# Second layer of a two-layer expert network: the gate as one Silu, low halves on VectorE, weight sets made across stage changes, first operands fetched in another order

## The chip, the cores and the metric

The kernel runs on one core of a Trainium2 chip. The metric is the device time of one execution in microseconds (us), as the median of several runs. The engines are TensorE (PE in the rows; its weight loads are PEld), VectorE (DVE), ScalarE (ACT), GpSimd (POOL) and SyncE (SP), which issues the DMAs of this kernel, in program order. Every engine takes its instructions in program order.

## The reference, cut to what matters

An attention block with 32 memory slots gives `x` of 4608 tokens by 512 features. Two layers of the same shape follow, 512 to 2048 and back to 512, in float32:

```python
def _moe_ref(x, w_in, w_out):       # first layer
    h = x @ w_in
    g = h * (1.0 / (1.0 + np.exp(-1.702 * h)))
    return g @ w_out

def _moe2_ref(x, w_in, w_out):      # second layer
    h = x @ w_in
    g = h * (1.0 / (1.0 + np.exp(-h)))
    return g @ w_out
```

## The kernel before, in words

Each float32 operand of a matmul is split in two: a rounded copy in the type F32R, written by ScalarE (the "high half"), and the remainder, a subtraction on VectorE or GpSimd (the "low half"). A product is then three matmuls (`PASSES`, L316). The last three of the four stages multiply 2x2 block matrices with seven products in place of eight; `ORDER` (L399) gives their order 1, 2, 6, 5, 7, 3, 4, and the price is sums and differences of operand blocks.

Four stages follow each other, in a schedule written out by hand: `at(slot, when, fn, ...)` enters a step in a table and `emit` issues it at its place, so the order of the calls is the order on each engine.

1. **First stage** (L336, 128 steps): attention and the first layer's first product. The gate is a Tanh on ScalarE and a multiply on VectorE (L338, L339). `store` (L342) sends each tile `g` to the DRAM tensors `g1s`. In the last twelve steps, from `ZS` (L956), `b_fetch` (L680) fetches the first operands of the second stage from `g1s`: 11 calls, 16 transfers of 384 KB, one call a step. `swap_pools` has by then given the attention's room to the pools `xst` (tags `xr0` to `xr6`) and `xp` (tags `x1` to `x7`).
2. **Second stage**, `middle` (L999; products at L734, 168 steps of 12 matmuls): the first layer's second product. `b_make` prepares the operand of step t+3 while step t runs (`AHEAD`, L970). At its start the pool `moe`, with the tiles that the last stores still read, is freed, and `b4` and `wm` take its room: `b_make(2)` writes into it. 12 weight sets are fetched (`wb_fetch`, L392). Towards its end, from L = T - 28, it makes weight sets of the third stage: `w_fetch` (L435) brings four 256 KB pieces into a staging tile (`wst` in the pool `wm`, or the tags `xr0` to `xr4`), and `w_make` forms sums (`w_sum`, L445), the high half (`w_hi`, L470) and the low half (`w_low`, L473). A set of weights for one chunk c has 7 of these. Then `x_fetch`, `x_comb` and `x_split` bring, combine and split the third stage's first operands (`xr` to `xq`).
3. **Third stage**, `step1` (L544; products at L521): the second layer's first product, 48 rounds n (`NG1`) of seven products of 6 matmuls, in 6 blocks of 384-token pairs with 8 rounds each. A round has seven places k. Copies of banks go to tiles `e` (L554, L571, L582), VectorE adds the second products (L408), `tanh` (L528) writes a tile `gq` on ScalarE, and `close` (L532) forms (tanh(h) + 1) * h on VectorE and stores the result to the DRAM tensors `gs`. The weights carry a factor one half, so h is half the true value. The operands of the next block are combined and split around the change of blocks (L1070 to L1077), in part on GpSimd. `c2_part` (L795) converts the raw `w_out` weights beside it, five small operations on ScalarE, VectorE and GpSimd for each of 16 pieces. In the last block the weight sets of the fourth stage are made (`spread`, L1052), odd low halves on GpSimd.
4. **Fourth stage** (L637, 168 steps of 18 matmuls): the second layer's second product. `r_fetch` (L591) fetches its operands from `gs`, `a_prep` (L614) splits them three steps ahead (`make`, L1101).

Before the first step of the fourth stage the pools `ps3`, `ps_y` and `m3` of the third are freed, and its PSUM pool `ps4` (4 buffers of two banks) takes the banks. In the kernel before, `x` (three buffers) is the first tag of `ps3` and `y1` the second.

Of the kernel before, what the change touches and what calls it, by code (L numbers as in the profile page):

```python
# [21 lines left out]
def attn_moe_moe(ctx: ExitStack, tc: tile.TileContext, q, k, v, phi, w1i, w1o, w2i, w2o, out):  # L22
# [24 lines left out]
    ones = const.tile([128, 1], F32)  # L47
    w2s = dram.tile([128, 2, 16, 512], F32, name="w2s")
# [465 lines left out]
    e1, e2, xb, y2, gq = {}, {}, {}, {}, {}  # L514
# [10 lines left out]
    def e_tile():  # L525
        return pools["m3"].tile([128, HB], F32, tag="e", name="e", bufs=6)

    def tanh(key, h):  # L528
        t = gq[key] = pools["m3"].tile([128, HB], F32, tag="gq", name="gq", bufs=8)
        nc.scalar.activation(out=t, in_=h, func=ACTF.Tanh)  # L530
# [13 lines left out]
    def step1(n, k):  # L544

        new, old = n < NG1, n > 0
        if k == 0 and new:
            xb[n] = pools["ps3"].tile([128, 512], F32, tag="x", name="xb", bufs=3)[:, :HB]
            prod1(n, 1, xb[n], True)
            e1[n] = e_tile()  # L550
        if k == 0 and old:
            tanh((n - 1, 1, 1), e2[n - 1, 2])
        if k == 0 and new:
            nc.scalar.copy(out=e1[n], in_=xb[n])  # L554
        if k == 0 and old:
            close(n - 1, 1, 1, e2.pop((n - 1, 2)))
        if k == 1 and new:
            y1 = pools["ps3"].tile([128, 512], F32, tag="y1", name="y1")[:, :HB]
            prod1(n, 2, y1, True)
            add(nc.vector, e1[n], e1[n], y1)  # L560
            tanh((n, 0, 0), e1[n])
# [10 lines left out]
        if k == 3 and old:  # L572
            close(n - 1, 0, 1, e2.pop(n - 1))
# [40 lines left out]
    def a_prep(b, i, p, then):  # L614
# [5 lines left out]
        pool, tag = (("xp", "x1"), ("xp", "x2"), ("wm", "wst"), ("m4", "op2"))[k]  # L620
# [20 lines left out]
    def o_tile():  # L641
        return pools["m4"].tile([128, TT, 256], F32, tag="o", name="o4", bufs=5)
# [356 lines left out]
    def middle():  # L999
# [25 lines left out]
        for i, k in ((6, 23), (5, 24), (7, 25), (1, 26), (2, 27)):  # L1025
# [15 lines left out]
    def second_layer():  # L1041
# [4 lines left out]
        pools["ps_y"] = tc.alloc_tile_pool(name="ps_y", bufs=1, space=PSUM, side="right", reuse_waits="tile")  # L1046
        pools["m3"] = tc.alloc_tile_pool(name="m3", bufs=1, reuse_waits="tile")
# [120 lines left out]
```

## Time and profile before

| | |
|---|---|
| median of 3 runs | 1538.79 us (1536.07 to 1541.72) |
| profiled execution: its own time | 1541.98 us |
| its span, first to last instruction | 1540.2 us |
| granted TensorE clock, mean | 0.98 |
| busy share of the span: PE, DVE, ACT, POOL | 93%, 76%, 51%, 29% |

The span is cut into stages by the first and last matmul of each line. "Busy" is the time in which an engine ran instructions; "idle before" is the time an engine waited ahead of a group, with the instruction that ended the wait. PEclk is the share of its full clock that TensorE was granted. Start times count from the span's start.

### The profile page before, as it was taken

Reading aid. Unit: us, or ns where it says so; the run is one execution under the profiler, and the core shown is the slowest. Engines: PE = TensorE matmul, PEld = TensorE weight load, DVE = VectorE, ACT = ScalarE, POOL = GpSimd, SP = SyncE. Lnnn points to the kernel's source line nnn. Section 1 sums busy time; section 2 is a strip of 40 time slices with the busy share of each in tenths; the row PEclk is TensorE's granted clock in tenths of the full one; section 3 lists DMA queues with packets and bytes.
Section 4 is the critical chain, followed back from the end, with each engine's and each line's share of the span. In section 5 each row is a group of like instructions: output and inputs, shape, how many; then the busy total and the mean of one; then the engine's idle time right before and its main releaser. Section 6 shows DMA issues by size and latency. Waiting matters only on the chain.

```text
span 1540.2 us, 27551 instructions
## 1 busy us (share of the span) xinstructions
PE 1429.7 (93%) x10432; PEld 1346.2 (87%) x10432; DVE 1164.3 (76%) x1601; ACT 792.6 (51%) x1351; POOL 439.3 (29%) x292
## 2 busy tenths in 40 slices
PE   5579898889989999999989999999997999999998
PEld 3447777677779999999989999999997999999998
DVE  5777767676758888887987776767788788787875
ACT  3445656555634554554555655665564444444443
POOL 2322636363400011011002233333322044053150
PEclk9799999999999999999999999999998999999999
DMA  9657787867686366366233645455465515425230
GB/s 250 195 159 234 222 246 233 267 196 225 241 313 229 100 228 233 108 226 222 88 121 124 201 166 209 147 203 188 156 201 194 186 39 188 141 76 196 98 119 31
DMA packets 234438, 277.07 MB, mean 180 GB/s; under 512 B 52033, under 2 KB 218945, under 8 KB 234305
## 3 DMA queue, kind: packets, MB, share of 16 engines
q1 hardware_dynamic: 234304, 275.31, 54.6%
q8 instruction: 82, 1.34, 0.3%
q14 instruction: 52, 0.42, 0.1%
HBM read 166.20 MB, written 109.05 MB: 179 GB/s over the span
## 4 chain that ended last, share of the span: by engine, by line
PE 66%; DVE 7%; DMA 5%; issue 4%; ACT 3%; POOL 3%; SPq 1%; DVEq 0%; ACTq 0%; POOLq 0%
PE p L637 24%; PE pb L734 20%; PE xb L521 9%; PE y L521 6%; PE h L336 5%; DMA g1s<-g 4%; POOL xq L411 1%; PE a L239 1%; DVE op L411 1%; DVE pm L145 1%; DVE g L339 1%; DVE wq L411 1%; ACT g L338 1%; DVE e L408 1%; ACT gq L530 1%
## 5 line engine op out<-in xcount | busy, mean ns | idle before, releaser
L637 PE MATMUL p<-wq,op 128*128 128x256 f32 x3024 | 362.1, 283 | 4.8 <-DVE gq L535 4.8
L637 PEld LDWEIGHTS p<-wq,op 128*128 128x128 f32 x3024 | 361.9, 192 | 5.2 <-DVE gq L535 5.2
L734 PE MATMUL pb<-op,wq 128*128 128x384 f32 x2016 | 355.9, 338 | 9.3 <-ACT op L713 5.6
L734 PEld LDWEIGHTS pb<-op,wq 128*128 128x128 f32 x2016 | 352.6, 189 | 12.4 <-ACT op L713 6.3
L411 DVE TENSOR_TENSOR op<-rr,op 128x768 fp32r<-128x768 f32 x216 | 247.9, 1157 | 67.4 <-ACT op L622 41.8
L336 PE MATMUL h<-attnT,slab 128*128 128x288 f32 x1536 | 240.9, 310 | 17.6 <-DVE g L339 8.6
L336 PEld LDWEIGHTS h<-attnT,slab 128*128 128x128 f32 x1536 | 217.3, 196 | 45.3 <-DVE g L339 21.6
L521 PE MATMUL xb<-xq,wq 128*128 128x384 f32 x1152 | 219.2, 338 | 14.0 <-ACT e L554 5.6
L521 PEld LDWEIGHTS xb<-xq,wq 128*128 128x128 f32 x1152 | 199.9, 188 | 21.5 <-ACT e L554 8.7
L339 DVE SCALAR_TENSOR_TENSOR g<-g,h 128x288 f32<-128x288 f32 x256 | 106.9, 448 | 87.9 <-ACT g L338 86.8
L411 DVE TENSOR_TENSOR op<-r,op 128x768 fp32r<-128x768 f32 x120 | 131.3, 1101 | 54.7 <-ACT op L622 31.2
L521 PE MATMUL y<-xq,wq 128*128 128x384 f32 x864 | 165.7, 336 | 0.7 <-ACT e L582 0.7
L338 ACT ACTIVATE g<-h 128x288 f32<-128x288 f32 x256 | 99.0, 413 | 127.7 <-PE h L336 67.0
L813 POOL TENSOR_TENSOR c<-c 128x512 int32<-128x512 int32 x32 | 55.6, 1739 | 348.7 <-DVE c L810 140.8
L622 ACT CAST op<-rr 128x768 fp32r<-128x768 f32 x120 | 99.7, 835 | 107.1 <-PE p L637 81.4
L521 PEld LDWEIGHTS y<-xq,wq 128*128 128x128 f32 x864 | 151.1, 188 | 1.0 <-ACT e L582 1.0
L535 DVE SCALAR_TENSOR_TENSOR gq<-gq,e 128x384 f32<-128x384 f32 x144 | 113.2, 790 | 39.2 <-ACT gq L530 34.8
L530 ACT ACTIVATE gq<-e 128x384 f32<-128x384 f32 x144 | 75.3, 525 | 110.5 <-DVE e L408 108.0
L713 ACT CAST op<-rr 128x768 fp32r<-128x768 f32 x96 | 79.5, 833 | 71.5 <-PE pb L734 43.3
L408 POOL TENSOR_TENSOR rr<-rr,r 128x768 f32<-128x768 f32 x22 | 52.7, 2424 | 214.6 <-DMA r<-gs 214.6
L713 ACT CAST op<-r 128x768 fp32r<-128x768 f32 x72 | 60.0, 834 | 54.7 <-PE pb L734 44.8
L411 POOL TENSOR_TENSOR wq<-wst,wq 128x512 fp32r<-128x512 f32 x46 | 62.1, 1354 | 86.0 <-ACT wq L470 64.9
(110 smaller groups left out, 1541.2 us busy)
## 6 DMA issues: line engine op xcount, KB each, us to landing
g1s<-g SPq DMA_DIRECT2D x128, 288.0 KB, 4.3
gs<-gq SPq DMA_DIRECT2D x192, 192.0 KB, 2.1
rr<-g1s SPq DMA_DIRECT2D x60, 384.0 KB, 6.2
rr<-gs SPq DMA_DIRECT2D x60, 384.0 KB, 5.7
r<-g1s SPq DMA_DIRECT2D x36, 384.0 KB, 4.1
r<-gs SPq DMA_DIRECT2D x36, 384.0 KB, 6.1
xs<-eb SPq DMA_DIRECT2D x24, 384.0 KB, 3.1
xr<-xs SPq DMA_DIRECT2D x24, 384.0 KB, 4.6
```

Of the source, the lines that this page charges most:

```text
L336: nc.tensor.matmul(out=h, lhsT=w[:, wi, g, f0:f0 + 128], rhs=x[:, xi, g * HS:(g + 1) * HS], start=(g == 0 and n == 0), stop=(g == 1 and n ...
L338: nc.scalar.activation(out=t[:, u], in_=h, func=ACTF.Tanh, scale=0.851)
L339: nc.vector.scalar_tensor_tensor(out=t[:, u], in0=t[:, u], scalar=1.0, in1=h, op0=ALU.add, op1=ALU.mult)
L408: eng.tensor_tensor(out=out, in0=a, in1=b, op=ALU.add)
L411: eng.tensor_tensor(out=out, in0=a, in1=b, op=ALU.subtract)
L521: nc.tensor.matmul(out=out, lhsT=w[:, s, wi, f0:f0 + 128], rhs=x[:, s, xi], start=(start and s == 0 and k == 0), stop=(s == 1 and k == 2), ...
L530: nc.scalar.activation(out=t, in_=h, func=ACTF.Tanh)
L535: nc.vector.scalar_tensor_tensor(out=t, in0=t, scalar=1.0, in1=h, op0=ALU.add, op1=ALU.mult)
L622: nc.scalar.copy(out=t[:, :, 0], in_=s)
L637: nc.tensor.matmul(out=out[:, d], lhsT=t[:, u, gi, d * 128:(d + 1) * 128], rhs=w[:, u, wi], start=(start and d != 1 and p == 0 and u == 0 ...
L713: nc.scalar.copy(out=t[:, :, 0], in_=s)
L734: nc.tensor.matmul(out=out[:, d, :HB], lhsT=w[:, u, wi, d * 128:(d + 1) * 128], rhs=t[:, u, gi], start=(start and p == 0 and u == 0 and n ...
```

## The change

- The gate becomes one ScalarE operation: `gate` computes Silu with scale 2.0 of the same h. `close` keeps only the store. The Tanh's partner on VectorE is gone. One Silu of a [128, 1] tile is issued early in `middle`.
- `gq` has 5 buffers (8 before), `e` 5 (6 before), the output tile `o` 3 (5 before). The fourth stage's third operand buffer has a pool of its own, `op` (before: the tile `wst`). `y1` is the first tag of `ps3`.
- In the third stage every low half and `x_comb` runs on VectorE; GpSimd did some of them before.
- Weight sets: chunk 1 is made in the third stage's rounds 0 to 2 (before: at the end of the second stage), chunks 2 and 3 behind it, chunk 0 at half the pace. For the fourth stage, six of chunk 3's seven sets are made in that stage's steps 0 to 22 (`"last"`). The staging tiles change places.
- First operands: `b_fetch` has 9 calls in the first stage's last steps, with gaps, and two calls, (3, 2) and (2, 3), at the start of `middle`. `r_fetch` puts its blocks into other tags and all its first calls come before the fourth stage. The sums of the first block (`SUMS`) are spread over steps 5 to 9.
- `x_split(0, 3)` moves into the second stage's last step, `x_split(0, 4)` to the first round's place 3, on VectorE.

```diff
+    def gate(key, h):
+        t = gq[key] = pools["m3"].tile([128, HB], F32, tag="gq", name="gq", bufs=5)
+        nc.scalar.activation(out=t, in_=h, func=ACTF.Silu, scale=2.0)
...
-    def close(n, i, j, h):
+    def close(n, i, j):
         t = gq.pop((n, i, j))
-        nc.vector.scalar_tensor_tensor(out=t, in0=t, scalar=1.0, in1=h, op0=ALU.add, op1=ALU.mult)
...
         if k == 0 and new:
+            y1[n] = pools["ps3"].tile([128, 512], F32, tag="y1", name="y1")[:, :HB]
             xb[n] = pools["ps3"].tile([128, 512], F32, tag="x", name="xb", bufs=3)[:, :HB]
...
-            tanh((n - 1, 1, 0), xb[n - 1])
-            close(n - 1, 1, 0, xb.pop(n - 1))
+            gate((n - 1, 1, 0), xb.pop(n - 1))
+            close(n - 1, 1, 0)
...
-        pool, tag = (("xp", "x1"), ("xp", "x2"), ("wm", "wst"), ("m4", "op2"))[k]
+        pool, tag = (("xp", "x1"), ("xp", "x2"), ("op", "op"), ("m4", "op2"))[k]
...
-    BF = [(0, 0), (0, 1), (0, 2), (1, 0), (1, 2), (2, 0), (2, 1), (3, 0), (2, 2), (2, 3), (3, 2)]
-    for n in range(len(BF)):
-        at(ZS + n, "d", b_fetch, 0, *BF[n])
+    BF = [(0, 0), (0, 1), (0, 2), (1, 0), (1, 2), (2, 0), (3, 0), (2, 1), (2, 2), (3, 2), (2, 3)]
+    for n, z in enumerate((0, 1, 2, 4, 6, 7, 8, 9, 10)):
+        at(ZS + z, "d", b_fetch, 0, *BF[n])
...
+    SUMS = {5: ((0, 0),), 6: ((0, 1), (1, 0), (1, 1)), 7: ((2, 0),), 8: ((2, 1), (3, 0)), 9: ((3, 1),)}
...
+        for x in BF[9:]:
+            b_fetch(0, *x)
         b_make(2)
         b_make(3)
...
+        nc.scalar.activation(out=spare, in_=ones, func=ACTF.Silu)
...
-        at(L + 9, "b", w_fetch, 0, 1, "wst")
+        at(L + 14, "b", w_fetch, 0, 1, "wst")
         for k in range(7):
-            at(L + 2 + k, "b", w_make, 0, 0, k, nc.vector, nc.vector)
-            at(L + 12 + k, "b", w_make, 0, 1, k, nc.vector, nc.vector)
+            at(L + 1 + 2 * k, "b", w_make, 0, 0, k, nc.vector, nc.vector)
...
-        for i, k in ((6, 23), (5, 24), (7, 25), (1, 26), (2, 27)):
+        for i, k in ((6, 23), (5, 24), (7, 25), (1, 26), (2, 27), (3, 27)):
             at(L + k, "b", x_split, 0, i, nc.vector)
...
-                at1(*divmod(n + 1, 7), w_low, c, k, nc.gpsimd if k % 2 else nc.vector)
+                at1(*divmod(n + 1, 7), w_low, c, k, nc.vector)
...
-        x_split(0, 3, nc.vector)
-        x_split(0, 4, nc.gpsimd)
-        w_fetch(0, 2, "wst")
-        spread(0, 2, range(9, 23, 2))
-        w_fetch(0, 3, "xr")
-        spread(0, 3, range(23, 37, 2))
+        at1(0, 3, x_split, 0, 4, nc.vector)
+        at1(1, 0, w_fetch, 0, 2, "xr")
+        spread(0, 1, range(6, 20, 2))
+        spread(0, 2, range(20, 34, 2))
+        at1(3, 0, w_fetch, 0, 3, "wst")
+        spread(0, 3, range(34, 48, 2))
...
-                at1(*divmod(7 * n + k + 1, 7), x_low, b, i, nc.gpsimd if i in (1, 6, 7, 4) else nc.vector)
+                at1(*divmod(7 * n + k + 1, 7), x_low, b, i, nc.vector)
...
-        for c, k in enumerate((0, 14, 24, 38)):
-            at1(*divmod(n + k, 7), w_fetch, 1, c, ("wst", "xr")[c % 2])
-        for c in range(3):
-            spread(1, c, range(n + 14 * c + 9, n + 14 * c + 23, 2))
-        spread(1, 3, [n + k for k in (51, 52, 54, 56, 57, 59, 61)])
+        for c, k in enumerate((6, 11, 24, 38)):
+            at1(*divmod(n + k, 7), w_fetch, 1, c, ("xr", "wst")[c % 2])
+        for c, k in enumerate(((10, 12, 14, 16, 18, 20, 22), (24, 26, 28, 30, 32, 34, 36), (37, 38, 40, 42, 43, 45, 46))):
+            spread(1, c, [n + x for x in k])
+        at1(*divmod(n + 51, 7), w_sums, 1, 3, 0, nc.vector)
+        at1(*divmod(n + 52, 7), w_low, 3, 0, nc.vector)
+        for k, t in enumerate((0, 1, 9, 10, 11, 21)):
+            at(t, "last", w_sums, 1, 3, 1 + k, nc.vector)
+            at(t + 1, "last", w_low, 3, 1 + k, nc.vector)
...
-        for n, k, a in ((1, 3, (0, 2)), (1, 5, (1, 0)), (1, 6, (1, 2)), (0, 2, (2, 0)), (0, 4, (2, 2))):
+        for n, k, a in ((1, 0, (2, 0)), (1, 1, (3, 0)), (1, 3, (0, 2)), (1, 5, (1, 0)), (1, 5, (2, 1)), (1, 5, (3, 1)),
+                        (1, 6, (1, 2)), (0, 2, (2, 2)), (0, 4, (3, 2))):
             at1(NG1 - n, k, r_fetch, 0, *a)
...
-        at1(NG1, 2, make, 2)
+        at1(NG1, 4, make, 2)
...
-        for p in range(4):
-            r_fetch(0, 3, p)
         bank = {}
         for t, (b, i, p) in enumerate(seq):
             if t + AHEAD < len(seq):
                 make(t + AHEAD)
+            emit(t, "last")
```

## Rows read from the trace of the kernel before

**Rows 1.** Windows by stage: length, busy time (instructions) of each engine, PEclk, DMA share, GB/s.

```profile
432.50:797.60 365.10, 355.81 (x2018) 352.71 (x2017) 303.26 (x352) 183.93 (x242) 34.74 (x16) 0.99 0.53 180
797.60:1173.60 376.00, 356.58 (x2018) 348.31 (x2016) 281.90 (x440) 223.91 (x450) 120.85 (x71) 0.99 0.53 181
1173.60:1535.40 361.80, 361.76 (x3023) 361.77 (x3024) 277.68 (x245) 153.79 (x189) 103.26 (x42) 0.99 0.36 123
```

**Rows 2.** Chain that ended last, an undisturbed stretch of the third stage: start, us.

```profile
1012.81 2.08 PE xb L521 x12
```

**Rows 3.** Windows, from the first stage's end into the second.

```profile
436.90:441.70 4.80, 0.01 (x1) 0.02 (x1) 0.04 (x1) 0.90 (x2) 0.00 (x0) 0.99 0.96 319
441.70:446.00 4.30, 3.99 (x11) 3.59 (x12) 3.53 (x4) 2.13 (x3) 0.00 (x0) 0.50 1.02 386
```

**Rows 4.** Chain that ended last, at the start of the second stage.

```profile
436.74 3.99 DMA g1s<-g
...
440.80 0.84 ACT op L713
...
441.67 0.97 DVE op L411
```

**Rows 5.** Windows, the last 38 us of the second stage.

```profile
760.00:780.00 20.00, 17.34 (x95) 15.97 (x94) 16.21 (x22) 8.02 (x13) 0.00 (x0) 1.00 0.32 97
780.00:798.00 18.00, 16.47 (x92) 15.41 (x91) 18.00 (x22) 10.03 (x14) 0.00 (x0) 1.00 0.12 44
```

**Rows 6.** Windows of the third stage, about a block of eight rounds each.

```profile
797.60:858.60 61.00, 58.83 (x334) 57.20 (x333) 47.54 (x76) 36.38 (x74) 13.75 (x9) 1.00 0.50 167
858.60:919.70 61.10, 60.52 (x348) 59.88 (x346) 43.67 (x68) 35.82 (x71) 21.20 (x13) 1.00 0.54 181
...
980.80:1041.90 61.10, 59.02 (x337) 58.16 (x336) 43.47 (x68) 35.85 (x71) 21.18 (x13) 1.00 0.52 181
...
1103.00:1168.80 65.80, 60.08 (x331) 56.73 (x330) 55.95 (x92) 41.74 (x88) 19.67 (x14) 1.00 0.58 191
1168.80:1173.60 4.80, 0.04 (x1) 0.00 (x0) 4.71 (x7) 2.43 (x5) 2.69 (x2) 0.50 0.93 316
```

**Rows 7.** Timeline at the third change of blocks: start, us, instruction, idle before it.

```profile
977.14 2.22 POOL L411 TENSOR_TENSOR xq<-xr,xq 128x768 fp32r<-128x768 f32 x1 [0.78 <-ACT xq L504]
978.03 1.61 DVE L808 TENSOR_SCALAR c<-c 128x512 int32<-128x512 int32 x1
...
981.81 2.35 PE L521 MATMUL xb<-xq,wq 128*128 128x384 f32 x12 [1.00 <-ACT e L554]
```

**Rows 8.** Window, the first microseconds of the fourth stage.

```profile
1173.60:1178.00 4.40, 4.37 (x20) 4.37 (x21) 2.23 (x3) 1.47 (x3) 0.00 (x0) 0.50 1.05 389
```

**Rows 9.** Groups by line and form: count, busy us, mean ns, idle before, releasers.

```profile
L535 DVE SCALAR_TENSOR_TENSOR gq<-gq,e 128x384 f32<-128x384 f32 x144 | 113.2, 790 | 39.2 <-ACT gq L530 34.8 <-DMA gs<-gq 0.6
L535 DVE SCALAR_TENSOR_TENSOR gq<-gq,xb 128x384 f32<-128x384 f32 x48 | 26.4, 549 | 19.1 <-ACT gq L530 19.1
L530 ACT ACTIVATE gq<-e 128x384 f32<-128x384 f32 x144 | 75.3, 525 | 110.5 <-DVE e L408 108.0 <-DMA xr<-xs 2.3
L411 POOL TENSOR_TENSOR xq<-xr,xq 128x768 fp32r<-128x768 f32 x21 | 41.5, 1974 | 155.2 <-ACT xq L504 134.3 <-DVE e L408 15.6 <-DVE xq L411 5.3
L411 DVE TENSOR_TENSOR xq<-xr,xq 128x768 fp32r<-128x768 f32 x21 | 19.7, 947 | 0.9 <-ACT xq L504 0.9
L411 DVE TENSOR_TENSOR wq<-wst,wq 128x512 fp32r<-128x512 f32 x38 | 27.8, 731 | 4.3 <-ACT wq L470 4.3
L554 ACT COPY e<-xb 128x384 f32<-128x384 f32 x48 | 22.6, 472 | 0.0
L174 ACT ACT_TABLE_LOAD x1 | 1.3, 1283 | 5.9 <-DMA phi<-in_phi_dram 5.9
```

**Rows 10.** DMA issues, weight pieces: count, KB each, median us to landing.

```profile
wst<-w2s SPq DMA_DIRECT2D x32, 256.0 KB, 5.1
```

**Rows 11.** Tile gq: its stores' time from issue to landing, min/median/max.

```profile
DMA to landing us min/median/max: 1.8/2.1/7.3
```

More of the change, by code (lines that the diff above doesn't have):

```diff
@@ L47, in attn_moe_moe @@
     ones = const.tile([128, 1], F32)
+    spare = const.tile([128, 1], F32)
     w2s = dram.tile([128, 2, 16, 512], F32, name="w2s")
@@ L512, in x_split @@
         x_low(b, i, eng)
-    e1, e2, xb, y2, gq = {}, {}, {}, {}, {}
+    e1, e2, xb, y1, y2, gq = {}, {}, {}, {}, {}, {}
     def prod1(n, i, out, start):
@@ L525, in e_tile @@
     def e_tile():
[L526 to L530, printed above, removed]
-    def close(n, i, j, h):
+        return pools["m3"].tile([128, HB], F32, tag="e", name="e", bufs=5)
+    def gate(key, h):
+        t = gq[key] = pools["m3"].tile([128, HB], F32, tag="gq", name="gq", bufs=5)
+        nc.scalar.activation(out=t, in_=h, func=ACTF.Silu, scale=2.0)
+    def close(n, i, j):
         b, f = divmod(n, 8)
         t = gq.pop((n, i, j))
-        nc.vector.scalar_tensor_tensor(out=t, in0=t, scalar=1.0, in1=h, op0=ALU.add, op1=ALU.mult)
         c0 = (2 * b + j) * HB
@@ L551, in step1 @@
         if k == 0 and old:
-            tanh((n - 1, 1, 1), e2[n - 1, 2])
+            gate((n - 1, 1, 1), e2.pop((n - 1, 2)))
         if k == 0 and new:
@@ L555, in step1 @@
         if k == 0 and old:
-            close(n - 1, 1, 1, e2.pop((n - 1, 2)))
+            close(n - 1, 1, 1)
         if k == 1 and new:
[L558 to L561, printed above, removed]
+            prod1(n, 2, y1[n], True)
+            add(nc.vector, e1[n], e1[n], y1.pop(n))
+            gate((n, 0, 0), e1.pop(n))
         if k == 2 and old:
@@ L564, in step1 @@
             add(nc.vector, e2[n - 1], e2[n - 1], y2.pop(n - 1))
-            tanh((n - 1, 0, 1), e2[n - 1])
+            gate((n - 1, 0, 1), e2.pop(n - 1))
         if k == 2 and new:
-            close(n, 0, 0, e1.pop(n))
+            close(n, 0, 0)
         if k == 3 and new:
@@ L591, in r_fetch @@
     def r_fetch(b, q, p):
-        if q == 3 or (q == 0 and p < 2):
-            x = p if q else 5 + p
+        if q != 1 and p < 2:
+            x = (5, 0, 0, 2)[q] + p
             ts = {p: pools["xst"].tile([128, 2, HB], F32, tag=f"xr{x}", name="r")}
         else:
-            i = {0: (0, 6), 1: (5, 7), 2: (3, 4)}[q][p // 2]
+            i = ((6, 6), (5, 7), (3, 3), (4, 4))[q][p // 2]
             t = pools["xp"].tile([128, 2, 2, HB], F32, tag=f"x{i}", name="rr")
@@ L641, in o_tile @@
     def o_tile():
-        return pools["m4"].tile([128, TT, 256], F32, tag="o", name="o4", bufs=5)
+        return pools["m4"].tile([128, TT, 256], F32, tag="o", name="o4", bufs=3)
     def o_store(b, i, j, t):
@@ L976, in b_make @@
             b_fetch_after(b + 1, i, p)
-        if 6 <= t < 10:
-            add(nc.vector, rb[0, 2, t - 6], rb[0, 2, t - 6], rb[0, 3, t - 6])
-            sub(nc.vector, rb[0, 0, t - 6], rb[0, 2, t - 6], rb[0, 0, t - 6])
+        for p, k in SUMS.get(t, ()):
+            if k == 0:
+                add(nc.vector, rb[0, 2, p], rb[0, 2, p], rb[0, 3, p])
+            else:
+                sub(nc.vector, rb[0, 0, p], rb[0, 2, p], rb[0, 0, p])
     for t in range(2):
@@ L1046, in second_layer @@
         pools["ps_y"] = tc.alloc_tile_pool(name="ps_y", bufs=1, space=PSUM, side="right", reuse_waits="tile")
+        pools["op"] = ctx.enter_context(tc.tile_pool(name="opp", bufs=1, reuse_waits="tile"))
         pools["m3"] = tc.alloc_tile_pool(name="m3", bufs=1, reuse_waits="tile")
@@ L1095, in fetch_after @@
                     continue
-                if q == 3 or (q == 0 and p < 2):
+                if q != 1 and p < 2:
                     r_fetch(b + 1, q, p)
@@ L1104, in make @@
             fetch_after(b, i, p)
-            if 6 <= t < 10:
-                add(nc.gpsimd if t % 2 else nc.vector, ra[0, 2, t - 6], ra[0, 2, t - 6], ra[0, 3, t - 6])
-                sub(nc.vector, ra[0, 0, t - 6], ra[0, 2, t - 6], ra[0, 0, t - 6])
+            for p, k in SUMS.get(t, ()):
+                if k == 0:
+                    add(nc.vector, ra[0, 2, p], ra[0, 2, p], ra[0, 3, p])
+                else:
+                    sub(nc.vector, ra[0, 0, p], ra[0, 2, p], ra[0, 0, p])
         at1(NG1 - 1, 2, make, 0)
         at1(NG1 - 1, 4, make, 1)
-        at1(NG1, 2, make, 2)
+        at1(NG1, 4, make, 2)
         for n in range(NG1 + 1):
@@ L1116, in second_layer @@
                 emit(n, k)
-        assert not todo
+        assert all(k == "last" for _, k in todo)
         pools["ps3"].release()
```

4 lines of the change are left out of this document (2 added, 2 removed).

## The prediction

> **What bounds the kernel now.** I read the windows by stage first [rows 1]. In the fourth stage TensorE is busy for 361.76 of 361.80 us: 3024 matmuls at 0.1196 us, with nothing to gain. An undisturbed stretch of the third stage passes 12 matmuls in 2.08 us [rows 2], 0.1733 us each. At that pace the 2016 matmuls of the second and of the third stage need 349.4 us each; they take 365.1 and 376.0. So 15.7 and 26.6 us are lost there, and any gain is a part of these or of the first stage's end. The table of windows is then read as length minus matmuls times 0.1733.
>
> At the first stage's end the DMA engines are full (share 0.96 to 1.02) and TensorE stands still for 4.8 us [rows 3]. The chain says why [rows 4]: the last store of `g` lands 3.99 us after its issue, only then may `b_make(2)` write into the freed pool, and a cast (0.84) and a subtraction (0.97) follow. Behind the stop the granted clock is 0.50, the lower level of 1.2 GHz: 11 matmuls in 4.3 us where 25 would fit, 2.4 us lost [rows 3].
>
> The second stage's last 38 us pass 187 matmuls, worth 32.4 us: 5.6 lost [rows 5]. VectorE is the cause: in the last 18 us it is busy for all 18.00.
>
> In the third stage the loss lies in places [rows 6]: 3.1 us in the first window; 0.8 in the second; 2.7 in the fourth, and the third and fifth are its like; 8.4 in the sixth, which I take to hold a 2.7 of the same kind (the fifth change of blocks); 4.8 before the fourth stage. At a change of blocks a GpSimd low half takes 2.22 us, a VectorE operation beside it takes 1.61, and TensorE then waits for ScalarE's copy, which is queued behind a gate that waits for VectorE [rows 7]. The clock falls to 0.50 once more at the fourth stage's start: 20 matmuls in 4.4 us where 36.8 would fit, 2.0 us lost [rows 8].
>
> **The change part by part**, each term with its bounds.
>
> *VectorE and GpSimd in the third stage.* Gone from VectorE are 192 multiplies, 113.2 + 26.4 = 139.6 us [rows 9]. Added are 21 low halves of operands at 0.947 (19.9), 16 combinations of the same shape (15.2), 18 low halves of weights at 0.731 (13.2) and chunk 1's seven low halves and four sums (8.0); eight operations of chunk 3 leave (5.8). 281.9 [rows 1] becomes some 192, about 55% of the stage, and nearly all that stretched the rest on GpSimd is gone: only the conversion's adds stay.
>
> *The gate on ScalarE.* Silu is not in this trace. Below stands the copy of the same shape (472 ns), nearest the Tanh (525); I take 525, so ScalarE's work is unchanged. Above I allow the same difference again, 578: 0.2 us more a round, beside 35.85 busy in 61.1 [rows 6, 9].
>
> *Its table.* One load, 1283 ns [rows 9], on ScalarE, behind the casts of operands 2 and 3. From 440.80: two casts (1.68), the load, the small Silu (under 0.47), the next cast (0.84) and its subtraction (0.97) give 446.0; TensorE, restarted at 442.6 with two operands of 2.08 us each, wants it at 446.8. Cost 0, with 0.8 us to spare; 1.3 if that cover is gone. The Trainium skill, "ScalarE: Activation LUTs", section "What ACT_TABLE_LOAD costs", adds a drain of about 1.38 us to the same 1283; by that the operand comes 0.6 us late and the sum is 0.6 smaller.
>
> *First stage's end.* Two calls, three transfers of 0.393 MB, now queue on SP behind the last store: 1.18 MB at 319 to 386 GB/s [rows 3] is 3.1 to 3.7 us less ahead of it. I take **3**; 0 if TensorE itself then sets the stage's end, 7 if stop and slow clock both vanish (4.8 + 2.4). The 12 weight fetches stand behind them in the queue; their first reader is step 16, 33 us on, and the late operands' first reader is the sum issued in step 4, 8 us on.
>
> *Second stage's end.* Chunk 1's 11 VectorE operations (8.0 us) leave, one low half (0.95) comes: 7 us less against 5.6 lost. I take **4.5**, since the combinations and splits still come at the very end; bounds 0 and 5.6. Chunk 0's first sum follows its fetch by four steps, 8.3 us, for a landing of 5.1 [rows 10].
>
> *Third stage, first block.* Chunks 1 to 3 now fill it, without multiplies: **2** of 3.1, bounds -2 and 3.1.
>
> *Changes of blocks.* Lost now 0.8 + 4 x 2.7 = 11.6. What is late next is ScalarE: 13 places of 1.04 us around a change hold 6.5 us of copies and gates (3 x 0.47 + 4 x 0.525 a round) and seven casts (5.9 at the 0.84 of [rows 4]), 12.4 of 13.5 and the conversion's two besides; each gate still waits for a VectorE add. I keep 1 us for each of four changes and 0.5 for the first: **7**, bounds 3 and 11.
>
> *Last block.* 8.4 - 2.7 = 5.7 lost. VectorE loses its multiplies and most of chunk 3, but the change adds a wait: chunk 0's pieces are fetched at place 6 and summed at place 10, 4.2 us on, against a landing of 5.1. Behind that sum on VectorE stand the adds, behind these the gates and copies. I keep 1.5: **4**, bounds 0 and 5.7.
>
> *Into the fourth stage.* Its first bank now covers `y1` and a buffer read a round earlier, and the last gate reads its bank on ScalarE with no multiply behind. I leave 0.9 (a gate and the hand-overs) of 4.8: **3.9**, bounds 0 and 4.8. With so short a stop I take the clock not to fall: **2**, bounds 0 and 2.
>
> *At nothing.* The fourth stage gets six low halves, two sums and two adds, some 8 us of VectorE over 23 steps (66 us); it is busy for 277.68 of 361.80 [rows 1], which leaves 15. The earlier `r_fetch` calls wait on SP for tiles that products at that very place let go; the stores behind them have the ring below to cover them. Rings `e` and `o` come round only after their readers.
>
> **Sum:** 3 + 4.5 + 2 + 7 + 4 + 3.9 + 2 = 26.4, taken as 26. The profiled execution took 1541.98 us, its span 1540.2; the median of the runs, 1538.79, is 3.2 lower. I take the same 26 from the median: **1513 us**.
>
> **The rivals.**
>
> 1. *ScalarE's order binds further.* Copies and gates still alternate behind VectorE's adds, so changes and last block keep most of their loss: terms 1, 3.5 and 2 in place of 2, 7 and 4, and 2 less in front of the fourth stage with the clock falling still (2). That is 10.5 less: 1523. For it: the waits of [rows 7] end at a ScalarE copy, and ScalarE's work stays. Against: what made that copy late was a slowed VectorE.
> 2. *The stage change isn't loosened.* If the first product of the fourth stage still waits until the last readers of all banks and tiles have finished, and these stay as late, 3.9 + 2 fall away: 1519. Against: the last reader has no VectorE queue before it.
> 3. *The shorter ring, slower.* `gq` falls to five buffers; a buffer is wanted again 8 places, 8.3 us, after its gate. Stores land in 2.1 us as a rule, 7.3 at most [rows 11]. If landing and SP's queue together passed 8.3, the gate would stop and everything on ScalarE with it. At 9.3 each of 38 rounds of the ring would lose 1 us: 1551. It decides only from four times the usual landing on.
> 4. *Tables change to and fro, slower.* Were a copy not in Silu's table set, six switches a round, 288 in all, at 1283 ns would add 370 us to ScalarE's 223.9 in a stage of 376.0: at least 218 us more, some 1730. The trace has one load for Exp, Tanh, copies and casts together. The Trainium skill, same page, section "Table sets: the hidden batching unit", says that cheap functions such as copy are in every set; by that rule this falls away, and the trace's single load agrees as far as it goes.
>
> **How the numbers follow.** Forecast 0.60, rivals 0.20, 0.10, 0.05 and 0.02; 0.03 for a loss that I don't see. The terms' bounds lie 1 to 40 us below before, not all at one end together; 10 us below the forecast needs stop and slow clock gone at the first stage's end and most of the changes' 11.6. The range, 1503 to 1529, takes in rivals 1 and 2 with some of their spread. A measurement of this kernel can tell about 0.3%, 4.6 us, from no change: faster means under 1534.2. Faster 0.88 (forecast, rivals 1 and 2 but for 0.02 of their tails), same 0.04, slower 0.08.
>
> **What the changed profile would show.** A third stage of some 357 us with its transition, GpSimd busy under 30 us in it; windows at changes of blocks losing about 1 us, with a ScalarE copy as releaser; a stop under 1 us before the fourth stage and a clock of 1.00 behind it; the stop after the first stage still near 4.8 but 3 us earlier; VectorE no longer full at the second stage's end; two table loads in all; Silu at 525 ns. I am wrong if Silu takes over 600 ns, if gates wait for `gs` stores, or if TensorE's new idle time ends at VectorE's subtractions.

## The result, and the profile after

The changed kernel takes 1502.53 us (median of 6 runs, 1500.86 to 1506.63), the kernel before 1539.97 in the same comparison; the ratio is 0.9764, with a 95% interval of 0.9745 to 0.9783. From the 1538.79 of the first runs that is 36.3 us less; 26 were forecast. 1502.53 lies half a microsecond below the range that was given.

First the windows by stage of the changed kernel, with the columns of [rows 1] (length, busy time and instructions of PE, PEld, DVE, ACT, POOL, then PEclk, DMA share, GB/s).

```profile
432.00:790.20 358.20, 352.15 (x2018) 351.43 (x2017) 297.65 (x342) 183.00 (x238) 34.70 (x16) 0.99 0.55 188
790.20:1140.10 349.90, 349.73 (x2018) 349.25 (x2017) 193.14 (x303) 221.61 (x449) 23.31 (x16) 1.00 0.56 191
1140.10:1500.20 360.10, 360.10 (x3026) 360.04 (x3024) 277.53 (x254) 157.81 (x197) 99.14 (x40) 1.00 0.37 127
```

The third stage fell from 376.0 to 349.9 us and TensorE is busy in it for 349.73: nothing is left to gain there at this pace of matmuls. VectorE's 193.14 is what the sum of the prediction gave (192). The second stage fell by 6.9. The fourth fell by 1.7 by these windows, which are cut to a tenth and not quite at the same place, and by 2.0 from the start of its first matmul to the start of its last. Against [rows 6], the windows of the third stage:

```profile
790.20:851.00 60.80, 60.80 (x353) 60.80 (x352) 42.63 (x68) 42.05 (x86) 0.00 (x0) 1.00 0.53 175
851.00:912.00 61.00, 61.00 (x354) 61.00 (x353) 29.29 (x45) 37.43 (x77) 5.82 (x4) 1.00 0.54 187
...
1095.00:1140.00 45.00, 44.83 (x258) 44.35 (x258) 32.48 (x54) 31.77 (x66) 0.00 (x0) 1.00 0.67 219
```

The windows of 61 us with a change of blocks, from the second on, hold 354 matmuls each; the kernel before had 348 in the second and 336 or 337 in the others. GpSimd has the conversion alone. The last stop at the first stage's end got no shorter; windows, as in [rows 3]:

```profile
436.40:442.20 5.80, 0.06 (x2) 0.02 (x1) 0.85 (x3) 1.61 (x4) 0.00 (x0) 0.80 0.75 255
442.20:446.50 4.30, 3.99 (x11) 3.59 (x12) 3.16 (x4) 3.60 (x5) 0.00 (x0) 0.50 1.03 381
```

The chain that ended last, there (start, us, what):

```profile
429.79 7.06 DMA g1s<-g
...
438.24 2.96 DMA g1s<-g
...
441.30 0.84 ACT op L713
```

The stop is 5.74 us where it was 4.79, and the clock falls to its lower level behind it as before. A store issued at 429.79 lands 7.06 us later; a gate of the first stage waits for its buffer, and the last store goes out only at 438.24. But this stop is not the whole of the stage's end. TensorE's timeline from the attention's last group of matmuls to the second stage's restart, of the kernel before:

```profile
403.62 1.09 PE L239 MATMUL a<-w,kvT 64*32 64x512 f32 x16
...
428.99 3.75 PE L336 MATMUL h<-attnT,slab 128*128 128x288 f32 x24 [2.37 <-DVE g L339]
...
442.68 330.38 PE L734 MATMUL pb<-op,wq 128*128 128x384 f32 x1883 [0.31 <-DVE op L411]
```

and of the changed kernel:

```profile
405.83 1.09 PE L240 MATMUL a<-w,kvT 64*32 64x512 f32 x16
...
443.18 347.25 PE L734 MATMUL pb<-op,wq 128*128 128x384 f32 x1991 [0.31 <-DVE op L412]
```

This stretch takes 39.06 us before and 37.35 after. The kernel before stops three times in it (2.26, 2.37 and 4.79 us), the changed kernel twice (2.44 and 5.74): one stop is gone, the last grew, and the stretch is 1.7 us shorter. Groups by line of the changed kernel, for [rows 9]:

```profile
L531 ACT ACTIVATE gq<-e 128x384 f32<-128x384 f32 x144 | 75.7, 526 | 101.0 <-DVE e L409 100.8
L412 DVE TENSOR_TENSOR xq<-xr,xq 128x768 fp32r<-128x768 f32 x42 | 42.4, 1018 | 11.8 <-ACT xq L505 11.8
L1015 ACT ACT_TABLE_LOAD x1 | 1.3, 1283 | 0.0
```

Silu takes 526 ns, the Tanh's time. Its one load is the second and last of the run.

### The profile page after: what moved, and what is told of

The parts are those of the page before. It is cut to its first block, busy times and chain, and to the rows that moved or that the text cites. A ratio compares the mean times of both kernels' runs of the same rounds, so it can differ in the third digit from the quotient of the medians.

```text
span 1504.8 us, 27070 instructions
## 1 busy us (share of the span) xinstructions
PE 1418.9 (94%) x10432; PEld 1345.6 (89%) x10432; DVE 1069.2 (71%) x1466; ACT 794.1 (53%) x1353; POOL 336.9 (22%) x235
## 4 chain that ended last, share of the span: by engine, by line
PE 78%; DMA 4%; DVE 3%; ACT 1%; issue 1%; POOL 1%; SPq 0%; ACTq 0%; DVEq 0%; POOLq 0%
PE p L637 24%; PE pb L734 23%; PE xb L522 13%; PE y L522 10%; PE h L337 5%; DMA g1s<-g 4%; PE a L240 1%; DVE g L340 1%; ACT g L339 1%; DVE pm L146 1%; PE a L192 1%; PE a L228 0%; POOL wst L96 0%; DVE nat L254 0%; ACT slab L297 0%
## 5 line engine op out<-in xcount | busy, mean ns | idle before, releaser
L734 PE MATMUL pb<-op,wq 128*128 128x384 f32 x2016 | 352.3, 336 | 6.0 <-ACT op L713 5.7
L412 DVE TENSOR_TENSOR op<-rr,op 128x768 fp32r<-128x768 f32 x204 | 233.3, 1152 | 57.8 <-ACT op L622 35.5
L522 PE MATMUL xb<-xq,wq 128*128 128x384 f32 x1152 | 215.7, 336 | 0.0
L412 DVE TENSOR_TENSOR op<-r,op 128x768 fp32r<-128x768 f32 x132 | 141.6, 1077 | 63.1 <-ACT op L622 37.2
L622 ACT CAST op<-rr 128x768 fp32r<-128x768 f32 x108 | 89.8, 838 | 92.0 <-PE p L637 77.2
L713 ACT CAST op<-rr 128x768 fp32r<-128x768 f32 x96 | 80.0, 835 | 73.0 <-PE pb L734 44.7
L409 DVE TENSOR_TENSOR e<-e,y 128x384 f32<-128x384 f32 x96 | 52.7, 552 | 60.8 <-PE y L522 54.1
L713 ACT CAST op<-r 128x768 fp32r<-128x768 f32 x72 | 60.2, 836 | 54.5 <-PE pb L734 43.5
L409 POOL TENSOR_TENSOR r<-r 128x768 f32<-128x768 f32 x10 | 23.4, 2364 | 274.5 <-DMA r<-gs 274.4
L622 ACT CAST op<-r 128x768 fp32r<-128x768 f32 x60 | 50.1, 836 | 61.1 <-PE p L637 48.2
```

The source lines that it names most:

```text
L409: eng.tensor_tensor(out=out, in0=a, in1=b, op=ALU.add)
L412: eng.tensor_tensor(out=out, in0=a, in1=b, op=ALU.subtract)
L522: nc.tensor.matmul(out=out, lhsT=w[:, s, wi, f0:f0 + 128], rhs=x[:, s, xi], start=(start and s == 0 and k == 0), stop=(s == 1 and k == 2), ...
L622: nc.scalar.copy(out=t[:, :, 0], in_=s)
L713: nc.scalar.copy(out=t[:, :, 0], in_=s)
L734: nc.tensor.matmul(out=out[:, d, :HB], lhsT=w[:, u, wi, d * 128:(d + 1) * 128], rhs=t[:, u, gi], start=(start and p == 0 and u == 0 and n ...
```

## The experiments

The first 404 us or so run the same instructions in all these kernels, but reach the attention's last group of matmuls between 398.3 and 405.8 us after the start. So kernels are compared by stage: the third stage is taken from its first matmul to the fourth stage's first (350.0 us in the changed kernel, where the window above reads 349.9), the stretch at the first stage's end from the start of the attention's last group to the second stage's restart.

Two theories for the third stage: **A**, it was freed because VectorE lost its multiplies; **B**, because GpSimd left.

| kernel | us | ratio to before | third stage, us |
|---|---|---|---|
| before | 1538.1 to 1540.5 | | 376.0 |
| changed | 1502.53 | 0.9764 | 350.0 |
| changed, Tanh and multiply back | 1517.15 | 0.9864 (0.9841 to 0.9886) | 362.1 |
| before, Silu alone | 1526.42 | 0.9923 (0.9894 to 0.9952) | 366.4 |
| changed, GpSimd back | 1513.16 | 0.9834 (0.9815 to 0.9853) | 358.3 |
| changed, GpSimd beside | 1516.88 | 0.9843 (0.9814 to 0.9872) | 364.0 |

**Tanh and multiply back**, without the early Silu; a cut of the edit:

```diff
-        nc.scalar.activation(out=t, in_=h, func=ACTF.Silu, scale=2.0)
+        nc.scalar.activation(out=t, in_=h, func=ACTF.Tanh)
...
+        nc.vector.scalar_tensor_tensor(out=t, in0=t, scalar=1.0, in1=h, op0=ALU.add, op1=ALU.mult)
```

> The changed kernel with the gate as Tanh on ScalarE and the multiply on VectorE again; all else of the change stays. Theory A (the third stage was freed because VectorE lost its 192 multiplies, so that the gates and copies on ScalarE no longer wait behind them): some 106 us of VectorE work come back, the third stage with its transition goes from 349.9 us to 360 or more, the time from 1502.5 to 1512 or more. Theory B (it was freed because GpSimd left the third stage: its low halves were slow and stretched VectorE's operations beside them): the stage stays below 353 us and the time below 1506.

12.1 of the 26.1 us come back, as A has it. They come in small pieces, most in the first and last block, where weights are made; the windows of this run:

```profile
786.10:847.00 60.90, 59.99 (x339) 58.58 (x338) 53.42 (x94) 39.69 (x82) 0.00 (x0) 1.00 0.51 170
847.00:908.00 61.00, 61.00 (x348) 60.97 (x347) 45.04 (x77) 36.11 (x72) 5.85 (x4) 1.00 0.52 179
...
1091.00:1146.20 55.20, 53.83 (x298) 51.09 (x296) 49.54 (x89) 35.08 (x74) 0.00 (x0) 1.00 0.63 206
```

VectorE is busy for 53.42 of 60.90 and 49.54 of 55.20 there, and TensorE waits for ScalarE's copies, which are queued behind gates that wait for VectorE. One such place: a gate waits 0.80 us for VectorE's add, and the weight load behind the next copy 1.00 us for that copy (idle time before in brackets):

```profile
1103.56 0.53 ACT L531 ACTIVATE gq<-e 128x384 f32<-128x384 f32 x1 [0.80 <-DVE e L409]
...
1105.03 2.03 PEld L522 LDWEIGHTS xb<-xq,wq 128*128 128x128 f32 x12 [1.00 <-ACT e L572]
```

**Silu alone**, the kernel before with the gate and its early table load changed, and nothing else:

```diff
-        nc.scalar.activation(out=t, in_=h, func=ACTF.Tanh)
+        nc.scalar.activation(out=t, in_=h, func=ACTF.Silu, scale=2.0)
...
-        nc.vector.scalar_tensor_tensor(out=t, in0=t, scalar=1.0, in1=h, op0=ALU.add, op1=ALU.mult)
```

> The kernel before with the gate as one Silu and its early table load, nothing else. Theory A: most of the third stage's 26 us come with this alone, the stage falls from 376.0 to 360 us or less, the time to 1524 or less. Theory B: GpSimd's low halves still stretch VectorE and stand in front of the products at the changes of blocks, the stage stays at 368 us or more, the time at 1531 or more.

366.4 lies between the two: 9.6 us come with Silu alone, so neither theory stands by itself. At the fifth change of blocks the timeline of this run still reads:

```profile
1092.53 2.35 PE L522 MATMUL xb<-xq,wq 128*128 128x384 f32 x12 [0.41 <-ACT e L554]
...
1096.99 2.21 PE L522 MATMUL xb<-xq,wq 128*128 128x384 f32 x11 [0.68 <-POOL xq L412]
```

**GpSimd back**, the changed kernel with the third stage's odd low halves and combinations on GpSimd:

```diff
-                at1(*divmod(n + 1, 7), w_low, c, k, nc.vector)
+                at1(*divmod(n + 1, 7), w_low, c, k, nc.gpsimd if k % 2 else nc.vector)
...
-                at1(*divmod(7 * n + k + 1, 7), x_low, b, i, nc.vector)
+                at1(*divmod(7 * n + k + 1, 7), x_low, b, i, nc.gpsimd if i in (1, 6, 7, 4) else nc.vector)
```

with the like for `x_comb`.

> The changed kernel with GpSimd's low halves of operands and weights and its combinations back in the third stage. Theory A: VectorE has room, the stage stays below 353 us, the time below 1506. Theory B: losses of 2 to 3 us at each of the five changes of blocks return, the stage goes to 360 us or more, the time to 1512 or more. If both theories are needed, the products at the changes wait for a GpSimd low half by some 1 us each, and the stage takes 353 to 358.

358.3, just above the upper end of the value for "both are needed". The first block, with weights made on both engines, loses nothing (60.90 busy of 60.90); the last four changes of blocks lose as with Silu alone, by the same two waits. The first block's window and the third change of this run:

```profile
788.10:849.00 60.90, 60.90 (x353) 60.90 (x352) 38.59 (x56) 42.16 (x86) 15.80 (x12) 1.00 0.53 175
```

```profile
966.26 2.35 PE L522 MATMUL xb<-xq,wq 128*128 128x384 f32 x12 [0.40 <-ACT e L555]
...
970.73 2.18 PE L522 MATMUL xb<-xq,wq 128*128 128x384 f32 x11 [0.69 <-POOL xq L412]
```

So GpSimd's leave clears the changes of blocks, and with the rest of the change in place GpSimd does no harm in the first block. That Silu by itself clears the first and the last block is not shown: with Silu alone the first block's window still holds 342 matmuls in 61.00 us (353 in 60.90 here), and TensorE still stops for 0.69, 0.91 and 2.39 us at the third stage's end. What is left there falls to the weight sets' new places and the other edits, together with Silu.

**GpSimd beside.** Is it that GpSimd's own low halves come late, or that GpSimd slows VectorE? This kernel has all low halves on VectorE and lets GpSimd do four of them a change once more, into a buffer that nobody reads; a cut of the edit:

```diff
+                if i in (1, 6, 7, 4):
+                    at1(*divmod(7 * n + k + 1, 7), lambda b, i: sub(nc.gpsimd, beside, xr[b, i], rd(xt[b, i][:, :, 0])), b, i)
                 at1(*divmod(7 * n + k + 1, 7), x_low, b, i, nc.vector)
```

> The changed kernel with four extra subtractions on GpSimd at each of the five changes of blocks, of the same operands and at the same places as GpSimd's low halves in the kernel before, whose results nobody reads; VectorE keeps all low halves. If the harm of GpSimd was that it stretches VectorE's operations beside it, the waits for ScalarE's copies return (0.4 us a change or more) and the third stage goes from 349.9 to 352 or more. If the harm was only that GpSimd's own low halves came late, nobody waits for these, and the stage stays at 350 to 351.

364.0: worse than with GpSimd's parts back. Nothing but GpSimd's own next subtraction waits for the extra ones (4.2 us, once), so slowing VectorE is harm enough. The timeline at the second change of blocks:

```profile
898.70 5.09 POOL L412 TENSOR_TENSOR beside<-xr,xq 128x768 fp32r<-128x768 f32 x2 [11.62 <-issue]
...
899.76 2.33 DVE L412 TENSOR_TENSOR xq<-xr,xq 128x768 fp32r<-128x768 f32 x1 [0.19 <-ACT xq L505]
...
902.01 2.07 DVE L808 TENSOR_SCALAR c<-c 128x512 int32<-128x512 int32 x1
...
906.18 0.52 ACT L531 ACTIVATE gq<-e 128x384 f32<-128x384 f32 x1 [3.86 <-DVE e L409]
...
907.12 2.35 PE L522 MATMUL xb<-xq,wq 128*128 128x384 f32 x12 [2.15 <-ACT e L555]
```

VectorE's subtraction takes 2.33 us, 0.95 alone; the shift of one tensor by a constant takes 2.07, 0.42 alone; GpSimd's own are slowed too (5.09 for two, 1.85 at best for one). The gate then waits 3.86 us for VectorE's add and TensorE 2.15 for the copy behind it. The times of single operations say how the slowing comes about:

```profile
909.53 2.56 POOL L412 TENSOR_TENSOR beside<-xr,xq 128x768 fp32r<-128x768 f32 x1 [2.71 <-ACT xq L505]
...
910.95 1.97 DVE L412 TENSOR_TENSOR xq<-xr,xq 128x768 fp32r<-128x768 f32 x1 [0.57 <-ACT xq L505]
...
913.10 1.85 POOL L412 TENSOR_TENSOR beside<-xr,xq 128x768 fp32r<-128x768 f32 x1 [1.00 <-DMA gs<-gq]
...
913.30 2.46 DVE L412 TENSOR_TENSOR xq<-xr,xq 128x768 fp32r<-128x768 f32 x1
```

VectorE's two subtractions began 1.4 and 0.2 us after GpSimd's, and both ended 0.8 us after GpSimd's had ended (912.92 against 912.09, 915.76 against 914.95). That is what taking turns looks like, and not the sharing of a rate: a short VectorE operation pays for all that is left of GpSimd's long one. The Trainium skill, "GPSIMD Engine Reference", section "Key points", says that GpSimd shares its interfaces to SBUF, the on-chip memory, with VectorE and that VectorE's instructions with two SBUF inputs, or in a mode with two ports, contend with it; the subtraction's 2.33 agrees with the first, and the shift, with one tensor input, would be of the second kind, which no row here tells. The page has no size for it.

**Chunk 1 back in the second stage**, with chunk 0 at its old pace:

```diff
-        at(L + 14, "b", w_fetch, 0, 1, "wst")
+        at(L + 9, "b", w_fetch, 0, 1, "wst")
...
-            at(L + 1 + 2 * k, "b", w_make, 0, 0, k, nc.vector, nc.vector)
+            at(L + 2 + k, "b", w_make, 0, 0, k, nc.vector, nc.vector)
+            at(L + 12 + k, "b", w_make, 0, 1, k, nc.vector, nc.vector)
...
-        spread(0, 1, range(6, 20, 2))
```

> The changed kernel with weight chunks 0 and 1 made in the second stage at the old places (chunk 1 no longer in the third). If VectorE's load of 11 operations at the second stage's end was what cost 5 to 6 us there, that loss returns: the second stage goes from 358.1 to 363 us or more, the third stays at 350. If the second stage gained by the other edits (sums of the first block spread, operands fetched in another order), it stays below 360.

1510.39 us, ratio 0.9819 (0.9798 to 0.9840). The second stage takes 363.8, the third 350.0. From the restart to the third stage's first matmul this run takes 354.0 us, the changed kernel 347.1, the kernel before 354.9. TensorE's stops at the second stage's end, from this run's timeline, are those of the kernel before to 0.03 us (0.83, 0.55, 1.29, 1.28, 0.25):

```profile
768.48 0.44 PE L734 MATMUL pb<-op,wq 128*128 128x384 f32 x1 [0.83 <-ACT op L713]
769.47 2.43 PE L734 MATMUL pb<-op,wq 128*128 128x384 f32 x12 [0.55 <-DVE op L412]
773.19 2.43 PE L734 MATMUL pb<-op,wq 128*128 128x384 f32 x12 [1.29 <-DVE op L412]
776.91 4.71 PE L734 MATMUL pb<-op,wq 128*128 128x384 f32 x24 [1.29 <-DVE op L412]
781.84 10.51 PE L734 MATMUL pb<-op,wq 128*128 128x384 f32 x59 [0.22 <-DVE op L412]
```

The changed kernel has no stop there of a quarter of a microsecond or more, though VectorE is nearly as full as before:

```profile
760.00:790.00 30.00, 30.00 (x175) 30.00 (x174) 29.17 (x34) 15.61 (x20) 0.00 (x0) 1.00 0.35 115
```

The third stage took chunk 1 in for nothing.

**y1 behind x**, the two tags of `ps3` in their old order:

```diff
-            y1[n] = pools["ps3"].tile([128, 512], F32, tag="y1", name="y1")[:, :HB]
             xb[n] = pools["ps3"].tile([128, 512], F32, tag="x", name="xb", bufs=3)[:, :HB]
+            y1[n] = pools["ps3"].tile([128, 512], F32, tag="y1", name="y1")[:, :HB]
```

> The changed kernel with x again the first tag of the third stage's PSUM pool and y1 behind it. If this order is what lets the fourth stage begin without a stop, its first matmul waits again for the last gate, which ends 0.7 us after it began in the changed kernel's trace: a stop of 0.7 to 1.0 us at the stage change, the clock at 1.00 behind it, the time 1 us longer. If the stop went with the VectorE queue alone, there is none (under 0.2 us).

One run, 1505.57 us. The stop is back, a little under the value set for it; this run's timeline:

```profile
1139.08 21.20 PE L637 MATMUL p<-wq,op 128*128 128x256 f32 x176 [0.63 <-ACT gq L531]
```

The third stage with its transition takes 350.7, so the order is worth 0.8 us. With `y1` first, the changed kernel's fourth stage starts before the last gate:

```profile
1140.23 5.02 PE L637 MATMUL p<-wq,op 128*128 128x256 f32 x41
...
1140.48 0.49 ACT L531 ACTIVATE gq<-xb 128x384 f32<-128x384 f32 x1
```

**Chunk 3 back in the third stage:**

```diff
-        at1(*divmod(n + 51, 7), w_sums, 1, 3, 0, nc.vector)
-        at1(*divmod(n + 52, 7), w_low, 3, 0, nc.vector)
-        for k, t in enumerate((0, 1, 9, 10, 11, 21)):
-            at(t, "last", w_sums, 1, 3, 1 + k, nc.vector)
-            at(t + 1, "last", w_low, 3, 1 + k, nc.vector)
+        spread(1, 3, [n + k for k in (51, 52, 54, 56, 57, 59, 61)])
```

> The changed kernel with all of chunk 3 of the fourth stage's weights made in the third stage, as before, on VectorE. VectorE has room in the last block now that its multiplies are gone: theory A and B together say that the third stage stays at 350 to 351 us. If moving six sets into the fourth stage was needed, stops of 1 us and more appear in the last round and the stage takes 352 or more.

One run, 1504.60 us; 351.2 in the third stage, between the two values. The move is worth 1.2 us there, and the fourth stage takes the six sets for nothing (359.8 us with them, 360.6 without, from its first matmul's start to its last's).

**All fetches early.**

```diff
-    for n, z in enumerate((0, 1, 2, 4, 6, 7, 8, 9, 10)):
+    for n, z in enumerate(range(11)):
...
-        for x in BF[9:]:
-            b_fetch(0, *x)
```

> The changed kernel with all 11 fetch calls of the second stage's first operands in the first stage's last steps, one a step, as before (in the new order). If the two moved calls free the DMA engines for the last stores, their return makes the stretch from the attention's last matmul to the second stage's restart longer: from 37.3 us (36.8 to 37.4 in the four runs with the new order) to 38 to 39, the two values of the runs with the old order. If the moved calls do nothing, it stays at 37.3 within 0.5.

The stretch is 38.79 us: the two moved calls, with the gaps between the others, shorten it by 1.4. (Eight runs with the changed order gave 36.79 to 37.35, the kernel before 39.06, the one with Silu alone 38.14.) The whole, 1504.60 us at 0.9783 (0.9762 to 0.9804), can't be told from the changed kernel's.

**Fetches later**, six calls behind the last stores:

```diff
-    for n, z in enumerate((0, 1, 2, 4, 6, 7, 8, 9, 10)):
+    for n, z in enumerate((0, 1, 2, 4, 6)):
...
-        for x in BF[9:]:
+        for x in BF[5:]:
```

> The changed kernel with six fetch calls (eight transfers) behind the last stores in place of two (three transfers). If the stop after the first stage is there because the last stores land behind fetches in the DMA engines, two more megabytes out of their way shorten the stretch from the attention's last matmul to the restart from 37.3 to 34 us or less, the stop from 5.7 to 3 or less, and the time to 1499 or less. If the stop hangs on something else, or the late operands now make VectorE wait at the first sums, the restart or the steps behind it are as late as before and the time stays at 1502 or above.

The stretch falls to 33.80, the stop to 2.10. TensorE's timeline, the attention's last group and the restart:

```profile
401.96 1.09 PE L240 MATMUL a<-w,kvT 64*32 64x512 f32 x16
...
434.77 0.44 PE L734 MATMUL pb<-op,wq 128*128 128x384 f32 x1 [2.10 <-ACT op L713]
435.76 347.15 PE L734 MATMUL pb<-op,wq 128*128 128x384 f32 x1991 [0.55 <-DVE op L412]
```

So the last stores do land late because fetches stand in front of them, and the change had moved too few. 1499.49 us, 0.9745 (0.9726 to 0.9763); 1499 or less was expected, so the time alone does not settle it, the stretch does. Run **again** beside the changed kernel:

> The kernel with six fetch calls behind the last stores again, in one call with the changed kernel: 3 to 4 us below it, 1499.

> The changed kernel as it is, on the same chip as the two kernels with later fetches, for a comparison within one call: 1502 to 1504 us, third stage 349.9, stretch to the restart 36.8 to 37.4.

1501.17 against 1505.05: 3.9 us. The changed kernel came 1 us above its expected values; its third stage is 350.0, its stretch 37.30.

**Fetches later still**, seven calls, and the second stage's first sums a step later each:

```diff
-    for n, z in enumerate((0, 1, 2, 4, 6, 7, 8, 9, 10)):
+    for n, z in enumerate((0, 1, 2, 4)):
...
-        for x in BF[9:]:
+        for x in BF[4:]:
...
+    LATER = {6: ((0, 0), (0, 1)), 7: ((1, 0), (1, 1), (2, 0)), 8: ((2, 1), (3, 0)), 9: ((3, 1),)}
```

> As the run with six fetch calls behind the last stores, but with seven (ten transfers) there and the second stage's first sums one step later each. If stores still stand behind fetches, the stretch from the attention's last matmul to the restart falls from 33.8 to 32 or 33 us and the time by another 1 us. If the store's own landing (2.6 us), the cast and the subtraction are what is left, the restart stays at 33.8, and operand (1, 2), now fetched last, may make TensorE wait at step 6.

The stretch does not fall further (33.29; the second run of the kernel with six calls had 32.79). The last store now lands in 2.55 us; from the chain that ended last:

```profile
433.32 2.55 DMA g1s<-g
```

The stop does fall, to 0.26 us, and the clock stays at 1.00; window of this run and its restart:

```profile
437.00:443.00 6.00, 5.45 (x30) 5.20 (x31) 4.85 (x6) 5.06 (x8) 0.00 (x0) 1.00 1.00 359
```

```profile
436.86 0.44 PE L734 MATMUL pb<-op,wq 128*128 128x384 f32 x1 [0.26 <-ACT op L713]
437.85 345.67 PE L734 MATMUL pb<-op,wq 128*128 128x384 f32 x1991 [0.55 <-DVE op L412]
```

From the restart on, 1991 matmuls take 345.67 us where both runs with six calls took 347.2: the clock's share. This kernel has the lowest median of all: 1498.71 us (1497.7 to 1499.7), 0.9728 (0.9705 to 0.9750), and 6.3 us below the changed kernel run beside it, whose runs (1503.73 to 1505.46) do not overlap with its own. With the kernel of six calls they do (1495.4 to 1502.14), so the times don't tell these two apart.

## Where the prediction was right, and where its terms were wrong

The direction and the places were right; the size was not: the sum was 26 where the profiled pair shows 35.4 (span 1540.2 to 1504.8). Of these, 26.1 lie in the third stage with its transition, 7.8 between restart and end of the second (354.9 to 347.1), 2.0 in the fourth and 1.7 in the stretch at the first stage's end; 2.2 go off because this profiled execution reached that stretch later (405.83 against 403.62), by the scatter of the first 404 us. So the measured time fell just outside the range, on its fast side: that side had been drawn 10 us below the forecast, while the bounds of the terms together allowed more.

- **First stage's end: 3 predicted, 1.7 measured by the stretch, 1.4 when the calls are put back.** The bytes moved were right, and so was that they stand in front of the last stores. The error was to price them one for one at the DMA's rate. In the changed kernel seven transfers are still issued among the last stores from 424.29 on, and one store took 7.06 us to land. Five more transfers out of the way shorten the stretch by another 3.5 to 4.5 us (37.3 to 33.8 and 32.8), the next two by nothing. The last stop (5.74) and the low clock behind it stayed, as the text expected; that the stop would come 3 us earlier did not come true.
- **Second stage's end: 4.5 predicted, 5.7 to 6.9 measured.** The cause named, 11 operations of chunk 1, is shown: put back, they bring all five stops and the time (354.0 us from the restart to the third stage, against 347.1 in the changed kernel and 348.3 when it was run again). The reserve for the combinations and splits at the very end was not needed. But VectorE did not cease to be full: it is busy for 29.17 of the last 30.00 us, and what it does now comes in time. The rest of the 7.8 is no more than scatter: the clock stays low a little longer behind the restart in one run than in another (0.70 in the window of 446.0 to 450.0 before, 0.97 in that of 446.5 to 450.0 after).
- **Third stage, changes of blocks: 7 predicted, all 11.6 measured.** This is the step that failed: "What is late next is ScalarE". I kept 1 us for each change because ScalarE's work filled 12.4 of 13.5 us. It does nearly fill it, and TensorE doesn't wait; a window of the changed kernel at the second change:

```profile
900.00:913.50 13.50, 13.50 (x79) 13.50 (x79) 10.56 (x15) 11.27 (x22) 1.90 (x1) 1.00 0.48 167
```

ScalarE was late only because its gates waited for VectorE. Its work need not be done inside the 13.5 us either: in the order of the calls a low half is made four or five places before the product that reads it. Rival 1, which took the same step further, falls with it.
- **First block: 2 predicted, 3 measured; last block: 4 predicted, all 5.7.** For the first block nothing stood behind the 1.1 held back. For the last block 1.5 were kept for **the wait that the change adds** (chunk 0's pieces summed 4.2 us after their fetch). The wait is there: VectorE waits twice, 0.81 and 0.82 us, for the landing. TensorE has no stop there. VectorE, half idle, has the room.
- **Into the fourth stage: 3.9 predicted, 4.8 measured; clock: 2.0 and 2.0.** No stop at all. Rival 2 falls: with the tags in their old order the stop is 0.63 us, and in the kernel with Silu alone 2.39, waiting for the last gate. So the multiply that is gone takes 2.4 of the 4.8 and the order of the tags some 0.6 to 0.8; which of the other edits took the rest was not tried.
- **At nothing** held throughout: Silu at 526 ns, the sets in the fourth stage, the rings. One sum of it was wrong and did no harm: 23 steps of the fourth stage are 49.5 us (361.8 / 168 each), not 66, so VectorE had 11.5 us of room there and not 15, for some 8 us of work. Rival 3 falls: stores of `gq` land in 2.1 us, at most 7.7, and no gate waits for one. Rival 4 falls: two loads in all.
- **The table load** cost 1.28 us of ScalarE and nothing else; the changed kernel's timeline:

```profile
442.88 1.28 ACT L1015 ACT_TABLE_LOAD   x1
...
444.18 0.20 ACT L1015 ACTIVATE spare<-ones 128x1 f32<-128x1 f32 x1
444.29 1.55 ACT L713 CAST op<-rr 128x768 fp32r<-128x768 f32 x2
```

The Trainium skill's further 1.38 us of drain ("ScalarE: Activation LUTs", "What ACT_TABLE_LOAD costs") is not seen: the Silu starts 1.30 us after the load did, and the next cast 0.11 us behind it. The measurement decides: 1.28 us.

What stays open: how much of GpSimd's harm at the changes of blocks is its own lateness (0.68 us of waits end at it) and how much the slowing of VectorE can't be parted cleanly, since the extra work of the GpSimd-beside kernel is slowed by VectorE as well. Nor was any edit but Silu tried alone in the kernel before: Silu, GpSimd, tags and chunk 3 put back one at a time cost 12.1, 8.3, 0.8 and 1.2 us, 22.4 of 26.1, and Silu alone brings 9.6, so part of the gain needs several edits together or lies with edits that were not put back.

## What to carry to other kernels

An engine that is not full by its busy share can still be the cause, when work on it stands between two other engines in program order: take operations out of that chain (here one ScalarE function in place of a function and a multiply) and the copies queued behind it come on time. Offloading elementwise work to GpSimd beside VectorE can cost more than it takes away; check VectorE's longest durations, not its mean. Where a stage ends in stores that the next one waits for, issue so many of the next stage's fetches behind them that the last stores find none in front of them: a few behind are not enough. Look at the granted clock behind each stop too: here 11 matmuls passed in 4.3 us where 25 would have at the full clock. And compare kernels from a mark inside the run, stage by stage: the end of a stop can move because the run reached it later.

## What the runs showed of the hardware that was not expected

- A GpSimd subtraction of 128x768 stretches VectorE's from 0.95 to 2.33 us, a one-tensor shift from 0.42 to 2.07, and is stretched itself (1.85 to 2.5). VectorE's stretched subtractions end 0.8 us after GpSimd's, wherever they began.
- The granted clock fell to its lower level behind every stop of 2.1 us and more at the second stage's start, for part of the time behind the one of 1.16 (0.72 over 437 to 443 us, second run with six calls), and not behind the one of 0.26. In the third stage of the GpSimd-beside kernel three stops of 2.0 to 2.15 us left it at 1.00 and a fourth of 2.15 did not (12 matmuls in 3.91 us behind it, in 2.35 or 2.36 behind the others). So the length of a stop alone does not tell.
- Two profiled executions of the same first 404 us of instructions can differ by some 7 us (398.3 to 405.8), as much as several terms of the sum.
